# The third sequence's attention scores on the two row halves of TensorE, with a spread mask and a new order of work

## The chip, the core and the metric

The kernel runs on one core of one Trainium2 chip. Five engines work side by side and are tied together by semaphores: TensorE (PE, matmuls; PEld is its weight load), VectorE (DVE), ScalarE (ACT), GpSimd (POOL) and SyncE (SP, here only an issuer of DMA transfers; GpSimd issues others). Each engine carries out its own list of instructions in order. The metric is the device time of one execution in microseconds; the median of three runs before the change is 260.41 us (259.87 to 261.34).

## The reference

Attention over four sequences (batch 4), 8 heads, 768 positions, head dimension 64, with a selection of key chunks, followed by a feed-forward network with squared ReLU:

```python
k_min, k_max = min / max of k over each chunk of 32 keys        # 24 chunks
ub = sum_d maximum(q * k_min, q * k_max)                        # bound of a query on a chunk
ub = where(query_chunk >= chunk, ub, -1e9)
top_chunks = the 6 chunks with the largest ub, for each query
scores = q @ k.T / 8
mask = (chunk of key in top_chunks) & (query >= key)
attn = softmax(where(mask, scores, -1e9))
x = attn @ v                                                    # (3072, 512)
out = relu(x @ w_in) ** 2 @ w_out                               # 512 -> 2048 -> 512
```

## The kernel before

**Tiles.** A sequence has six tiles of 128 positions. The first tile of each of the four sequences (it has only four chunks, fewer than the six that are chosen, so that nothing is left out there) is handled by `first_attention`, and these four tiles share one feed-forward pass ("F"). The other five tiles of sequence b are handled by pairs of heads: pair p = 4 b + hp, so the third sequence (b = 2) is pairs 8 to 11 and the fourth pairs 12 to 15. After its four pairs each sequence has its own feed-forward pass: up groups (four matmuls into one PSUM bank, line 1186), a relu on ScalarE or VectorE (1193, 1195), a square on VectorE (1204), down groups (four matmuls, line 1217).

**Two ways of scoring.** In the old way (`stage_a`, `stage_b`), sequences 0 to 2 here, keys and queries are copied into `kqc` tiles with 64 + 24 rows: 64 of the head, and 24 that hold for each chunk a large negative number on the key side and, on the query side, whether the chunk is *not* selected. One matmul over 88 rows then yields scores that already carry the chunk mask. A head has five PSUM banks of 512 columns (`BANKS`), each filled by two matmuls (line 1026). ScalarE takes the exponential (1050), GpSimd or VectorE cuts the diagonal blocks to their triangle (1006, 1003), and TensorE multiplies by the values (1038). `stage_a` prepares this for a pair: key copies `kc`, chunk minima and maxima (line 862), query parts, query copies `qc`, bounds on TensorE (825, 827), the eight largest (833), the selection `selb` (892), its transpose `sT`, and four copies of it into the `kqc` rows.

In the new way (`stage_a_turned`, `score_banks`, `stage_b_turned`), sequence 3 here, the scores are taken straight from the transposed keys and queries: for each block one matmul over rows 0 to 63 for the first head of the pair and one over rows 64 to 127 for the second (line 1083), which run on the two row halves of the array. `score_banks` does two banks of both heads, 16 matmuls, in one burst. The mask comes another way: the selection is made as large or zero numbers on VectorE (946, 957), transposed by SyncE, written to DRAM (`seen`, line 967), and spread from there by four transfers over 32 partitions each (line 974) into a tile `mask`. GpSimd cuts the mask's diagonal blocks (1006), and VectorE takes the minimum of exponential and mask (`choose`, line 1130). The values matmul is line 1116.

For sequences 2 and 3 keys and queries come already transposed, by SyncE's transposing DMA from tiles that GpSimd has loaded; for these sequences the transposition of the selection is SyncE's too, in both ways of scoring.

**Order.** The program first lists all operations (1797), each with the engines that may run it. `SEQUENCE` is the list of their numbers in the order in which they are issued, with a letter (D, A, G) where an operation may run on more than one engine. So this list fixes the order on each engine and the choice between engines. `Plan.order` walks through it with a model of durations and DMA (`Transfers`); at run time the model's only trace is how the buffers are assigned and how many warm-up matmuls fill the gaps at the start. Due times and leads in `P` were used by the search that made the list; the kernel itself takes from `P` the number and order of the loads (which also numbers the operations) and which passes go by DMA.

**Buffers.** PSUM: one bank `tp`, three `ps`, two `av`, two `ff`. The up and down groups use `ff`. Eight `e` buffers hold exponentials until the values matmul has used them. Three large buffers `set` hold the two `kqc` sets, sequence 1's loaded keys and queries, and later the masks.

Of the kernel before, what the change touches and what calls it, by code (L numbers as in the profile page):

```python
# [9 lines left out]
F32 = mybir.dt.float32  # L10
# [36 lines left out]
4 0 23 1 131 2 18 6 20 8 62D 7 10A 19 150 5A 22 12A 134 136 9A 135D 21 11D 13A 24 14D  # L47
3A 25 132 133D 27 61D 17D 137 16 148 26 138 146 142 147D 31 149D 143 139 174 144 29
151 145 176 140 152 141 32 177D 156 153 188 175A 154 28 157 155 178 15A 158 179 159 33
162 180 190 163D 191A 30 189D 164 184 36 192 195 193D 34 160 196A 198 161D 201 46 197  # L50
199A 194 165 202A 200 185 35 170 181 186 203 166 187 37 182 171 183 172 167 173 40 286
206 168 280 169 207A 287 41 204 290D 205A 39 288 282A 211 289D 208 45 212D 281A 213
214 209D 284 215A 217 60 226 218A 283 51 223 210 285 42 227A 219 291 224A 343 292 220
44 216 345A 293 43 229 294 344A 225 295 221A 347 296 230A 52 235 298A 346 297A 54 232
300A 228 299A 236D 38 309 317 222 310 349 237 301 48 233A 238 350 302 351 47 313 352D
318 241 348 314 353D 50 239A 305 234 322 311G 354 306 240 303G 323 355 250 67 307D 356
242A 315D 326 55 357 251A 304 308 330 324D 358 327 312 316 319 49 252 334 325 243 359
335 244 53 363D 331 362D 361D 412 332G 245A 385 336G 413 338 386 247 328G 360D 56 339
231 415D 372 248A 59 368 253 414 369 320 416D 69 373 376 249 364 406 321 374G 365 380
370G 409 256 254A 366G 65 410 367 371 375 377 389 68 262 381 408D 390 411 329 246 401  # L60
397 407D 391G 333 417 378G 398 337 255 340 469 387G 341 418 393 399G 471A 257 66 419
342 402 379 382 64 420 263 394 421 395D 388 383 422 472 392 71 396 423A 400 403 258
424D 384 435 404 427 426D 264 425D 428 473 436 448 439 449 57 470D 431 259 440 405
429G 432 474 460 437D 441D 475 260A 72 443 476 430 461 265 261 477 433G 444 70 478D
452 480 453 434 268 73 481 479A 483 462D 456 58 482 464 457 269 484 78 465 458D 438
266A 485 442 731 104 486D 267 270 487D 732A 488D 75 489D 506 450D 490 734 507 498 454G
445 271 79 499 735 491 451 98 455 494 500D 459 733D 463 495 523 492G 466 446 511 74
524 467 274 447 512 468 81 272A 737 736 525D 515 739 519 496G 502 741D 520 493 77 497
275 738 503 105 740D 513G 516 742 85 504D 527 743 501 505 528 508 521D 794 517G 509
744 83 514 518 796A 522 526 510 529 276 117 530 99 745 795A 531 277 76 746 797 80 747  # L70
534 278A 63G 749D 535A 532 748D 750D 102 533A 584 760 751D 585A 764 798 539 765 768
542 540A 799 769 800 543D 578 86 761 802 536 90 579A 544 801 752 537A 572 541 82 753
766G 580 756 538 575 573A 803D 805 804D 576A 557 108 84 757 577 545 806 558A 857 574
754G 546A 807 548 762G 858A 89 777 549D 566 808 859A 560 550 547 781 94 809 773 561A
755 860 567A 551 778 758G 103 581 774 562 779G 759 568 763 582D 782 767 785 87 775D
# [65 lines left out]
1755 1753D 1764 1756D 1757 1716 1715 1719 1770 1720A 1765A 1721 1728 1717A 1737 1718  # L141
1771D 1773 1754 1772 1729D 1766 1779 1730 1738D 1758 1780 1759A 1760 1774 1739 1781
1782 1775 1783D 1776 1784 1785 1777D 1786 1778 1787 1788 1791 1789A 1792 1793 1794
1790 1795A 1796
"""


class Transfers:
# [11 lines left out]
    def run(self, queues, until):  # L160
        now = self.now
# [1161 lines left out]
```

## Time and profile before

| | |
|---|---|
| median of 3 runs | 260.41 us |
| profiled execution | 260.51 us |
| its span, first to last instruction | 258.8 us |
| granted TensorE clock | 0.998 |
| scores matmuls, old way (line 1026) | 240 matmuls, 40.6 us busy |
| scores matmuls, new way (line 1083) | 160 matmuls, 6.2 us busy |
| exponentials (lines 1050 and 1121) | 120 x 602 ns and 40 x 602 ns |
| old scores of the third sequence | first at 118.5, last at 165.1 us |
| new scores of the fourth sequence | first at 166.6, last at 205.2 us |

How to read it: "busy" is the time in which an engine had an instruction under way; matmuls are pipelined, and each one's record is longer than the step to the next one, so that the busy time of a group of matmuls is more than what the group adds to TensorE's list. The chain of waits is followed back from the last instruction, and shows what a piece of work really added. A row of a group gives line, engine, operation, names (result, then operands), shape, count, busy us, mean ns of one, and idle time of the engine just before with what ended it.

### The profile page before, as it was taken

Reading aid. Unit: us, or ns where it says so; the run is one execution under the profiler, and the core shown is the slowest. Engines: PE = TensorE matmul, PEld = TensorE weight load, DVE = VectorE, ACT = ScalarE, POOL = GpSimd, SP = SyncE. Lnnn points to the kernel's source line nnn. Section 1 sums busy time; section 2 is a strip of 40 time slices with the busy share of each in tenths; the row PEclk is TensorE's granted clock in tenths of the full one; section 3 lists DMA queues with packets and bytes.
Section 4 is the critical chain, followed back from the end, with each engine's and each line's share of the span. In section 5 each row is a group of like instructions: output and inputs, shape, how many; then the busy total and the mean of one; then the engine's idle time right before and its main releaser. Section 6 shows DMA issues by size and latency. Waiting matters only on the chain.

```text
span 258.8 us, 6699 instructions
## 1 busy us (share of the span) xinstructions
PE 248.7 (96%) x2482; PEld 159.2 (62%) x2482; DVE 202.3 (78%) x719; ACT 177.6 (69%) x352; POOL 113.6 (44%) x194
## 2 busy tenths in 40 slices
PE   8787999999999999999999999999999999999995
PEld 3555466656688666565687656656765654865543
DVE  4659999999999999999999984578978870674630
ACT  7666898598799999999997638766977630421201
POOL 8979899769855599431311304231032200010000
PEclk9999999999999999999999999999999999999999
DMA  9999999999999999994658214973993206120022
GB/s 124 128 163 162 181 171 183 180 163 160 135 177 174 159 132 128 169 123 101 85 166 182 36 25 109 206 91 117 196 188 57 85 11 153 20 81 3 7 93 103
DMA packets 117280, 31.89 MB, mean 123 GB/s; under 512 B 99840, under 2 KB 114944, under 8 KB 117248
## 3 DMA queue, kind: packets, MB, share of 16 engines
q0 software_dynamic: 77968, 16.00, 76.3%
q1 hardware_dynamic: 39280, 15.47, 31.4%
q8 instruction: 19, 0.31, 0.5%
q14 instruction: 13, 0.11, 0.2%
HBM read 32.77 MB, written 6.55 MB: 152 GB/s over the span
## 4 chain that ended last, share of the span: by engine, by line
PE 63%; DMA 14%; DVE 10%; POOL 8%; issue 2%; ACT 1%; POOLq 0%
PE py L1217 27%; PE ph L1186 20%; DMA w_in_sb<-in_moe_w_in_dram 6%; PE ps L1026 6%; PE av L1038 4%; DMA w_out_sb<-in_moe_w_out_dram 3%; DMA qt<-nt 3%; PE ps L1083 2%; DVE kr L862 2%; PE av L1116 2%; DMA nt<-in_q_dram 2%; POOL kn L574 2%; DVE kqc L389 1%; DVE h L1204 1%; POOL q L481 1%
## 5 line engine op out<-in xcount | busy, mean ns | idle before, releaser
L1186 PE MATMUL ph<-xT,w_in_sb 128*128 128x256 bf16 (+2 forms) x592 | 98.1, 304 | 1.6 <-DMA w_in_sb<-in_moe_w_in_dram 0.9
L1217 PE MATMUL py<-w_out_sb,h 128*128 128x512 bf16 (+2 forms) x400 | 93.4, 370 | 0.0
L1050 ACT ACTIVATE e<-ps 128x512 bf16<-128x512 f32 x120 | 66.4, 602 | 9.3 <-PE ps L1026 7.5
L1193 ACT ACTIVATE ht<-ph 128x256 bf16<-128x256 f32 (+2 forms) x102 | 45.1, 451 | 39.4 <-PE ph L1186 30.7
L1186 PEld LDWEIGHTS <-w_in_sb 128*128 128x128 bf16 x592 | 54.8, 97 | 26.0 <-issue 1.3
L1217 PEld LDWEIGHTS <-h 128*128 128x128 bf16 x400 | 37.0, 97 | 33.3
L1204 DVE TENSOR_TENSOR h<-ht 128x384 bf16<-128x384 bf16 (+2 forms) x148 | 46.4, 334 | 10.3 <-ACT ht L1193 9.5
L1006 POOL TENSOR_SCALAR_AFFINE_SELECT e<-e 128x128 bf16<-128x128 bf16 (+1 forms) x68 | 23.2, 352 | 44.5 <-ACT e L1050 44.1
L1026 PE MATMUL ps<-kqc 88*128 88x128 bf16 (+1 forms) x240 | 40.6, 272 | 0.0
L1195 DVE TENSOR_SCALAR ht<-ph 128x384 bf16<-128x384 f32 (+2 forms) x46 | 22.8, 497 | 15.4 <-PE ph L1186 14.6
L1038 PEld LDWEIGHTS <-e 128*128 128x128 bf16 x480 | 23.3, 97 | 6.0 <-POOL e L1006 0.2
L1026 PEld LDWEIGHTS <-kqc 88*128 88x128 bf16 x240 | 19.7, 97 | 10.7 <-DVE kqc L389 0.7
L1121 ACT ACTIVATE e<-ps 128x512 bf16<-128x512 f32 x40 | 21.2, 602 | 5.7 <-PE ps L1083 3.4
L1038 PE MATMUL av<-vn,e 128*128 128x65 bf16 x360 | 23.7, 193 | 0.1
L1006 POOL TENSOR_SCALAR_AFFINE_SELECT mask<-mask 128x256 bf16<-128x256 bf16 x20 | 9.1, 481 | 30.6 <-DMA mask<-seen 30.6
L387 ACT COPY ob<-py 128x512 f32<-128x512 f32 (+2 forms) x18 | 10.2, 564 | 14.2 <-PE py L1217 14.2
L1231 POOL DMA_DIRECT2D out_dram<-ob x10 | 5.6, 556 | 31.9 <-DVE ob L389 18.3
L733 DVE TENSOR_TENSOR x<-av,rc 128x320 bf16<-128x320 f32 (+1 forms) x40 | 18.8, 473 | 0.8
L1130 DVE TENSOR_TENSOR e<-e,mask 128x512 bf16<-128x512 bf16 x40 | 16.1, 438 | 1.6 <-ACT e L1121 1.6
L862 DVE TENSOR_REDUCE kr<-kT 128x24 bf16<-128x768 bf16 x16 | 14.7, 948 | 0.1
L567 POOL DMA_DIRECT2D vn<-in_v_dram x15 | 13.6, 911 | 0.3 <-PE av L1038 0.3
L833 DVE MAX8 m<-ubm 128x8 f32<-128x24 f32 x120 | 12.0, 168 | 0.1
(116 smaller groups left out, 319.5 us busy)
## 6 DMA issues: line engine op xcount, KB each, us to landing
mask<-seen SPq DMA_DIRECT2D x16, 336.0 KB, 6.4
out_dram<-ob SPq DMA_DIRECT2D x13, 256.0 KB, 2.3
out_dram<-ob POOLq DMA_DIRECT2D x10, 256.0 KB, 2.7
w_in_sb<-in_moe_w_in_dram POOLq DMA_DIRECT2D x4, 512.0 KB, 7.6
w_out_sb<-in_moe_w_out_dram POOLq DMA_DIRECT2D x4, 512.0 KB, 9.0
vn<-in_v_dram POOLq DMA_DIRECT2D x15, 128.0 KB, 6.6
nt<-in_q_dram POOLq DMA_DIRECT2D x10, 128.0 KB, 5.1
nt<-in_k_dram POOLq DMA_DIRECT2D x10, 128.0 KB, 6.4
```

Source lines behind the costliest of these rows:

```text
L733: return plan.op({"DVE": 0.06 + 0.00108 * D * n}, due, lambda _: nc.vector.tensor_mul(x(), av[:, :, 0:D], rc[:, 0:n].unsqueeze(2).to_broad ...
L862: nc.vector.tensor_reduce(kr[:, mm].rearrange("d (t c) -> d t c", c=128 // CH) if b >= BY_DMA else kr[:, mm], part(kT).rearrange("d t (c j ...
L1006: nc.gpsimd.affine_select(out=e, in_=e, compare_op=ALU.is_ge, fill=0.0, base=0, channel_multiplier=-1, pattern=[[0, n], [1, 128]])
L1026: nc.tensor.matmul(ps[:, 128 * c:128 * (c + nt)], lhsT=kqs(slice(0, KC), s, hh)[:, 128 * j:128 * (j + 1)], rhs=qss(slice(0, KC), s, hh)[:, ...
L1038: nc.tensor.matmul(av[:, t - 1], lhsT=e[:, 128 * c:128 * (c + 1)], rhs=value_tile(b, h, j), start=(i == 0 and c == 0), stop=(i == len(BANK ...
L1050: nc.scalar.activation(e.tile, ps.tile, ACT.Exp, scale=scale), [sc], [ps, e])
L1121: done = plan.op({"ACT": 0.487}, due + 0.5, lambda _: nc.scalar.activation(e.tile, ps.tile, ACT.Exp, scale=scale), [sc], [ps, e])
L1186: nc.tensor.matmul(ph.tile, lhsT=w_in_sb[:, ki, 128 * f:128 * (f + 1)], rhs=xT[:, c0 // 128:c1 // 128, ki], start=(ki == 0), stop=(ki == N ...
L1193: nc.scalar.activation(ht.tile, ph.tile, ACT.Relu)
L1195: nc.vector.tensor_scalar_max(ht.tile, ph.tile, 0.0)
L1204: {"DVE": 0.075 + w / 1920}, at[0] + P["h2"], lambda _: nc.vector.tensor_mul(h2[f][:, c0:c1], ht.tile, ht.tile), [op], [ht, h2[f]], port=T ...
L1217: nc.tensor.matmul(py.tile, lhsT=h2[f][:, 128 * t:128 * (t + 1)], rhs=w_out_sb[:, f, c0:c1], start=(f == 0), stop=(f == NFI - 1))
```

## The change

The third sequence (pairs 8 to 11) goes the new way, too: `MASKED` falls from 3 to 2. For this sequence there are then no key and query copies, no selection copies and no triangle on the exponentials; instead there are 4 more writes of the selection to DRAM, 16 more spreads of the mask, 20 causal selects of the mask on GpSimd, 40 minima on VectorE and 10 bursts of 16 score matmuls. The output is computed as before.

The bounds of the pairs that go the new way are put in `ff` instead of `tp`. The list of operations has 1787 entries, and `SEQUENCE` is a new one throughout, from its first entries on: the order of the loads, which engine takes which copy, relu and triangle, and where everything stands are new. The model of the transfers has one more constant (a lower rate in the first 10 us), and `P` has other values; several keys in it are read by nothing in the kernel.

```diff
@@ SEQUENCE: all of it replaced; its first line before and after
-4 0 23 1 131 2 18 6 20 8 62D 7 10A 19 150 5A 22 12A 134 136 9A 135D 21 11D 13A 24 14D
+4 0 19 1 131 2 17D 61D 20 18 6 7 21 136 5A 8 23 150 30 13A 15D 134 14A 12D 29 135A 16
...
     SHARED = ((6.2, 0.90), (9.0, 0.95), (1e9, 1.0))
+    EARLY = (10.0, 0.85)
     ISSUED = {True: 0.7, False: 1.3}
...
-            span = min([until - now] + [q[0][1] / rate for q in active])
+            if now < self.EARLY[0]:
+                rate *= self.EARLY[1]
+                until_then = self.EARLY[0] - now + 1e-9
+            else:
+                until_then = 1e9
+            span = min([until - now, until_then] + [q[0][1] / rate for q in active])
...
-             sel=2, loads='K1 Q1 Q3 K3 V0 V1 Q2 K2 i0 V2 k0 V3 q0 i1 k1 v2 q1 i2 '
-             'v0 i3 k2 q2 o1 o0 v1 o2 k3 o3 v3 q3')
...
+    P = dict(... later='q1 k1 v1 k2 v3 q2 k3 v2 q3', ... xt=(1, 2, 3), ub='ff', ...
+             loads='K1 Q1 V1 Q2 V0 K2 Q3 K3 i0 V2 k0 V3 q0 i1 k1 v2 q1 i2 v0 i3 k2 q2 '
+             'o0 v1 o2 k3 o1 o3 v3 q3', out=[1, 2], sel=2)
...
     BY_DMA = 2
-    MASKED = 3
+    MASKED = 2
...
-        ub = buffer("tp", [128, NS, 2, NC], F32, name="ub")
+        ub = buffer("ff", [128, NS, 2, NC], F32, name="ub")
```

Counted by engine from both lists, where they differ in number: on VectorE copies of the selection 26 and 10, triangles on exponentials 28 and 16, query copies 16 and 9, first-tile copies 7 and 2, output copies 7 and 4, FFN input copies 1 and 5, relus 46 and 43, minima 40 and 80; on GpSimd triangles on exponentials 68 and 48, on masks 20 and 40; on ScalarE key copies 16 and 8, relus 102 and 105, output copies 18 and 21; on SyncE spreads 16 and 32, writes of the selection 4 and 8.

In the new list GpSimd's first loads are the first tiles K1, Q1, V1, V0, a pair of k for sequence 0, Q3, K3, V2, K2, Q2, V3, and then the first quarter of w_in; before they were V0, Q1, K1, K3, Q3, V1, Q2 and then the first quarter of w_in. The third sequence's first burst stands after the last scores of sequence 1. Between the third sequence's first mask spread and its first minimum stand, on VectorE, the eight key reductions of the fourth sequence.

More of the change, by code (lines that the diff above doesn't have):

```diff
@@ L145 @@
+1767A 1768 1771 1775 1776 1772 1777 1773D 1778 1774 1781 1779A 1782 1783 1784 1780
+1785A 1786
 """
@@ L164, in run @@
             rate = self.RATE / len(active)
-            span = min([until - now] + [q[0][1] / rate for q in active])
+            if now < self.EARLY[0]:
[4 more added lines that the diff above has]
+            span = min([until - now, until_then] + [q[0][1] / rate for q in active])
             if len(active) > 1:
                 before, share = next(x for x in self.SHARED if now < x[0])
-                span = min([until - now, before - now + 1e-9]
+                span = min([until - now, until_then, before - now + 1e-9]
                            + [q[0][1] / rate / share for q in active])
```

200 lines of the change are left out of this document (95 added, 105 removed).

## Prediction

> **What bounds the kernel now.** First the totals and the slices, then the engines' busy time in three stretches.
>
> ```profile
> span 258.8 us, 6699 instructions
> PE 248.7 (96%) x2482; PEld 159.2 (62%) x2482; DVE 202.3 (78%) x719; ACT 177.6 (69%) x352; POOL 113.6 (44%) x194
> DMA  9999999999999999994658214973993206120022
> ...
> core 0: us, PE busy (x) PEld busy (x) DVE busy (x) ACT busy (x) POOL busy (x), PEclk, DMA share, GB/s
> 0.00:30.00 30.00, 23.95 (x236) 14.34 (x237) 19.83 (x80) 20.42 (x34) 26.14 (x38) 1.00 1.67 148
> 30.00:150.00 120.00, 119.14 (x1285) 80.84 (x1285) 115.83 (x437) 106.49 (x214) 72.02 (x122) 1.00 1.54 146
> 150.00:258.80 108.80, 105.64 (x963) 64.02 (x960) 66.66 (x204) 50.69 (x105) 15.40 (x35) 1.00 0.42 92
> ```
>
> TensorE is busy for 119.1 of the 120 us between 30 and 150, at a granted clock of 1.00. VectorE is busy for 115.8 of the same 120 and has only 4.2 us of room there; after 150 it has 108.8 - 66.7 = 42 us. So TensorE's work sets the end, and VectorE is right behind it in just the stretch where the third sequence's attention runs. The chain of waits says the same in its pieces (start, duration, what):
>
> ```profile
> 150.01 2.59 PE py L1217 x12
> ...
> 154.97 0.44 PE ps L1026 x4
> ...
> 167.24 2.70 PE py L1217 x12
> 169.94 0.55 PE ps L1083 x16
> ```
>
> It runs without holes along TensorE: FFN groups with score matmuls between them. A matmul taken out here is time gained, unless another engine makes TensorE wait.
>
> The profiled execution took 260.51 us: the span of 258.8 and 1.7 around it. The median of the three runs is 260.41, so I work from 260.5 and take off 0.1 at the end.
>
> **The scores.** x4 of L1026 is two heads' banks in the old form: 0.44 us, 0.22 a bank. The third sequence has 40 banks (4 pairs of heads, 2 heads, 5 banks): 8.8 us. x16 of L1083 is four banks in the new form, two heads on the two row halves: 0.55 us, and the twelve FFN matmuls in front of it take 2.70 instead of 2.59, so 0.11 more goes at the switch. Ten such bursts are 10 x 0.66 = 6.6 us. **Gain 2.2 us** on TensorE. The values matmuls, the bounds and the FFN stay as they are.
>
> The Trainium skill's page "TensorEngine Tiling (Array Packing)" (Theoretical Speedup) gives up to 2x where the contracted side is at most 64. By that the 8.8 us would become 4.4 and the sum would be 2.2 us lower than mine. The rows show 8.8 / 6.6 = 1.33x, and I go by the rows.
>
> **VectorE.** The rows, as line, operation, count, busy us, mean ns:
>
> ```profile
> L1130 DVE TENSOR_TENSOR e<-e,mask 128x512 bf16<-128x512 bf16 x40 | 16.1, 438 | 1.6 <-ACT e L1121 1.6
> L862 DVE TENSOR_REDUCE kr<-kT 128x24 bf16<-128x768 bf16 x16 | 14.7, 948 | 0.1
> L389 DVE COPY kqc<-sT 24x256 bf16<-24x256 bf16 (+1 forms) x26 | 7.7, 295 | 1.0 <-PE sT L392 0.4
> L759 DVE TENSOR_REDUCE kr<-kt 128x24 bf16<-128x768 bf16 x8 | 7.5, 945 | 0.0
> L1003 DVE TENSOR_TENSOR e<-e,tri 128x128 bf16<-128x128 bf16 (+1 forms) x28 | 6.9, 254 | 2.6 <-ACT e L1050 2.4
> L389 DVE COPY kqc<-qT 64x640 bf16<-64x640 bf16 x12 | 5.8, 484 | 0.1
> L389 DVE COPY ob<-py 128x512 f32<-128x512 f32 x7 | 4.8, 690 | 6.7 <-PE py L1217 6.7
> L892 DVE TENSOR_TENSOR selb<-ubm,m 128x240 bf16<-128x240 f32 x12 | 4.8, 401 | 0.1
> L946 DVE TENSOR_TENSOR selb<-ubm,m 128x48 bf16<-128x48 f32 (+2 forms) x16 | 3.1, 244 | 0.0
> L389 DVE COPY t<-T 128x512 bf16<-128x512 bf16 x7 | 2.9, 422 | 5.0 <-PE T L392 5.0
> L957 DVE TENSOR_SCALAR selb<-selb 128x168 bf16<-128x168 bf16 x4 | 0.8, 204 | 0.1
> ```
>
> Added: 40 mask minima, 40 x 16.1/40 = 16.1; the finer selection, 3.1 + 0.8 - 4 x 4.8/12 = 2.3. Removed, by counting the engine letters of both lists: copies of the selection on VectorE fall from 26 to 10 (-16 x 0.30 = -4.8), triangular products from 28 to 16 (-12 x 0.25 = -3.0), query copies from 16 to 9 (at 0.48 at most -3.4, some are a shorter form, I take -2.7), first-tile copies from 7 to 2 (-2.1), output copies from 7 to 4 (-2.1). Smaller shifts of the new list (more copies of FFN inputs on VectorE, fewer relus) I take as zero. **Net +3.7 us** on VectorE. Its room between 30 and 150 was 4.2, and it shrinks with what TensorE gains there, to about 2. So 3.7 - 2 = 1.7 us don't fit, unless the new order moves work out of the stretch. It does for some: both key reductions of the very first pair (2 x 0.95) now stand ahead of the first FFN groups, in the 30 - 19.8 = 10 us that VectorE had idle at the start. The price is 0 if that is used in full, 1.7 if not, and up to 4.2 if the little idle time is hand-overs that no order removes. I take 0.5.
>
> The bounds of sequences 2 and 3 move from the one tp bank of PSUM to the two ff banks, where the FFN groups rotate; each holds its bank for one bounds group and one add, about what an up group and its relu hold, eight times in all: price 0. The changed planner constants and due times act only through the list.
>
> ScalarE loses the third sequence's long key copies and gets other copies in return; its 40 exponentials remain, and with 106 of 120 busy it isn't the bound. GpSimd gives up 20 triangular selects on e for 20 on the mask; it has 48 us idle in the stretch, price 0, cover enough.
>
> **SyncE and the mask.** Added are 4 writes of the selection to DRAM and 16 transfers that spread it, and what GpSimd waits for:
>
> ```profile
> 133.37 0.38 SPq L967 DMA_DIRECT2D seen<-sT  x1
> 135.11 3.32 SPq L974 DMA_DIRECT2D mask<-seen  x4
> ...
> 144.85 1.95 POOL L1006 TENSOR_SCALAR_AFFINE_SELECT mask<-mask 128x256 bf16<-128x256 bf16 x4 [7.34 <-DMA mask<-seen]
> ...
> mask<-seen SPq DMA_DIRECT2D x16, 336.0 KB, 6.4
> L1006 POOL TENSOR_SCALAR_AFFINE_SELECT mask<-mask 128x256 bf16<-128x256 bf16 x20 | 9.1, 481 | 30.6 <-DMA mask<-seen 30.6
> DMA to landing us min/median/max: 4.4/6.4/9.2
> ```
>
> From the first of four spreads (135.11) to the start of GpSimd's causal selects (144.85) is 9.7 us; two selects at 0.46 make 10.7 before the first minimum can go. In the new list TensorE has between the first pair's first spread and its first minimum nine FFN down groups (0.86 each: 2.59 / 3), three bursts (0.66), and an up group, a bounds group and four values groups (together about 1.2): 10.9 us. VectorE has all eight key reductions of the fourth sequence there (8 x 0.94 = 7.5) and some 3 us of selections and normalisations besides, so the wait is filled. That fits with 0.2 to spare. The third pair has about as much; the other two have some 2 us more, though their spreads are issued further apart. Queued behind a late minimum on VectorE is everything: the squares of the FFN and the next bounds, and then TensorE. I take 0 for it, with 0 to 4 as bounds. The third sequence's selections were already turned by SyncE before, so nothing is added there; the next sequence's input transposes and the last key tile of sequence 3 queue behind the spreads, each 0.3 to 0.5 of issue, while sequence 1's FFN inputs are ready only after its last values.
>
> **The start.** The list is new throughout. Of its loads, the first quarter of w_in is now 13th of GpSimd's loads instead of 8th, with ten first tiles and two pairs of heads ahead of it instead of seven first tiles:
>
> ```profile
> 8.81 7.81 DMA w_in_sb<-in_moe_w_in_dram
> ...
> 22.00 7.61 DMA w_in_sb<-in_moe_w_in_dram
> ...
> k<-in_k_dram POOLq DMA_DIRECT2D x3, 128.0 KB, 4.0
> kn<-in_k_dram POOLq DMA_DIRECT2D x8, 80.0 KB, 6.5
> ...
> 23.04 4.10 PE L1186 MATMUL ph<-xT,w_in_sb 128*128 128x256 bf16 x24 [0.39 <-ACT xT L387]
> ```
>
> Between the two landings (16.62 and 29.61) the queue moved three first tiles, nine pairs and two weight quarters of 512 KB, 2128 KB, or 164 KB/us. The 544 KB more put the first quarter at 16.6 + 3.3 = 19.9. All four sequences' first-tile attention is ahead of it in the new list, so TensorE has then only FFN groups and one pair's transposes to do. The row of 24 holds four narrow up groups and two of twice their width, so 4.10 / 8 = 0.51 a narrow one; eight of these and about 1 us of transposes and bounds bring the new list to 19.9 + 4.1 + 1 = 25.0. The old list has its eight narrow groups done at 23.04 + 4 x 0.51 = 25.1. I take 0, and -1.0 to +1.2 as bounds.
>
> **Sum.** 260.5 - 2.2 (scores) + 0.5 (VectorE) + 0 (mask, start) = 258.8, less 0.1 against the median: **258.7 us**, its own range 257.2 to 260.0.
>
> **The rivals.**
> *VectorE becomes the pace* (260.4): the 1.7 us that don't fit are paid, with 0.5 more where TensorE stands for a hand-over: 260.5 - 2.2 + 2.2 - 0.1. For it speaks 115.8 of 120; against it that 42 us lie free after 150 and that the fourth sequence's preparation can slide there. The Trainium skill's page named above (PSUM Bottleneck) says that tiling speeds up TensorE and not the emptying of PSUM; the 40 exponentials and, added here, 40 minima after them would be that.
> *The masks come late* (263.5, slower): pairs one and three have under 1 us of slack between first spread and first minimum. If the four spreads take 13 us instead of 9.7, because sequence 3's tiles and sequence 1's input transposes share the 16 engines with them, each of the two stops VectorE and then TensorE for some 2.6 us: 260.5 - 2.2 + 5.2 = 263.5. It decides the sign from about 11.6 us on. For it: the landing of one spread goes from 4.4 to 9.2, and the slices from 110 to 129 us show DMA at 9, 4 and 6 tenths without any spread. Against it: at 136 to 142 us, with four spreads under way, it is 8 tenths and most of that is their own.
> *The new order wins more* (256.9): a start 1.0 earlier and no price on VectorE, 260.5 - 2.2 - 1.0 - 0.1 = 257.2, with some of the switch time hidden 256.9. For it: 6 of the first 30 us have no TensorE work; against it: the first weights come later, not earlier.
> *The new scores gain nothing*, being hidden: TensorE at 119.1 of 120 speaks against, and I give it no chance of its own.
>
> **How the numbers follow.** A measurement of this kernel can tell about 0.5% (1.3 us) from no change, so faster is under 259.1, slower over 261.7. Forecast 0.45 (of it 0.36 faster, 0.09 same), more 0.17 (faster), VectorE's pace 0.16 (0.01 faster, 0.13 same, 0.02 slower), late masks 0.22 (slower, some of it only to the bound: 0.20 slower, 0.02 same). That is 0.54, 0.24 and 0.22. The range leaves out the upper part of the late masks and the lower end of the third rival: 256.7 to 262.3.
>
> **What would show it.** Right: the old scores' line at 160 matmuls and the new scores' line at 320, in 20 bursts; TensorE still over 119 of 120 between 30 and 150; VectorE 3 to 5 us busier in total, with the minima of the third sequence starting within 0.3 us of the mask's last causal select. Wrong: TensorE's idle time ended by minima or by VectorE's squares between 100 and 150 (VectorE's pace, if VectorE shows no idle time there; late masks, if VectorE waits for GpSimd's select on the mask), four spreads over 11.6 us from first issue to last landing, or a first FFN group after 21 us with idle time behind it.

## The result, and the profile after

The changed kernel takes **268.24 us** (median of 4 runs, 267.63 to 268.65) against 260.23 for the kernel before in the same comparison (4 runs, 259.87 to 261.34): ratio 1.030, 95% interval 1.026 to 1.034. It is slower by 8.0 us, outside the predicted range. The span is 266.9 us, before 258.8.

First the totals and the queue of SyncE's transfers (packets, MB, share of the 16 engines) of the changed kernel. Its line numbers are 4 lower than before: 1186 is now 1182, 1217 is 1213, 1026 is 1022, 1083 is 1079, 1130 is 1126.

```profile
span 266.9 us, 6891 instructions
PE 249.8 (94%) x2539; PEld 159.0 (60%) x2564; DVE 205.4 (77%) x735; ACT 173.3 (65%) x347; POOL 115.7 (43%) x195
q1 hardware_dynamic: 50864, 21.11, 44.8%
```

Then the three stretches as before:

```profile
core 0: us, PE busy (x) PEld busy (x) DVE busy (x) ACT busy (x) POOL busy (x), PEclk, DMA share, GB/s
0.00:30.00 30.00, 23.57 (x235) 15.35 (x236) 20.34 (x78) 19.67 (x35) 26.80 (x39) 0.94 1.63 146
30.00:150.00 120.00, 117.59 (x1287) 77.77 (x1298) 114.60 (x415) 97.12 (x196) 70.40 (x117) 1.00 1.71 164
150.00:270.00 120.00, 108.68 (x1021) 65.86 (x1032) 70.45 (x245) 56.52 (x118) 18.50 (x40) 0.98 0.55 112
```

TensorE by its records stands still for 2.4 us between 30 and 150, where it stood for 0.9. Two waits make 1.2 of it (0.7 and 0.5); part of the rest can be matmuls that the trace lacks, since it has 1287 beside 1298 weight loads there. Its time behind 150 has grown by 8.1 us with the span, while its busy time there has grown by 3.0 only (105.64 before). VectorE is busy for 3.1 us more in all, but 1.2 us *less* between 30 and 150 (115.83 before): it has not become the pace. The 0.94 in the first stretch is a low granted clock behind a wait of 1.34 us for a first tile of v (the clock is the third number from the end):

```profile
17.80:21.20 3.40, 3.40 (x37) 2.56 (x36) 1.80 (x7) 1.08 (x2) 2.08 (x3) 0.50 1.84 164
```

It hardly moves the start: in e2_warm below, which starts in the same way and has no such stretch, the first FFN group begins at 21.27 us, here at 21.25.

What TensorE, VectorE and SyncE waited for (engine, line, releaser: total, times, longest):

```profile
PE ph L1182 <- DMA xT<-x: 3.3, 1, 3.3
...
PE av L1112 <- DVE e L1126: 1.2, 1, 1.2
...
PE ub L745 <- DVE qp L777: 0.7, 1, 0.7
...
DVE e L1126 <- POOL mask L1002: 1.9, 1, 1.9
DVE qp L777 <- DMA qt<-nt: 1.3, 1, 1.3
...
SPq L970 <- DMA seen<-sT: 14.1, 5, 5.5
SPq L963 <- DMA sT<-selb: 9.4, 3, 3.9
```

The three waits of TensorE shown here can be followed back to one kind of cause. The FFN input of sequence 2 (`xT`) comes late from SyncE. A value group waits for a minimum, which waits for GpSimd's select, which waits for the mask's spreads. The bound of pair 8 waits for VectorE, which waits for sequence 2's turned queries. All of these are transfers that SyncE issues. But the bound of pair 8 stands at 102.4 us, and the first spread of that pair goes out at 117.15, so the new spreads have no part in this wait. The list of transfers (KB each, median from issue to landing) of the changed kernel shows them slower:

```profile
mask<-seen SPq DMA_DIRECT2D x32, 336.0 KB, 6.7
seen<-sT SPq DMA_DIRECT2D x8, 64.0 KB, 4.7
xT<-x SPq DMA_TRANSPOSE x15, 3.5
qt<-nt SPq DMA_TRANSPOSE x10, 7.4
sT<-selb SPq DMA_TRANSPOSE x8, 5.3
```

and that of the kernel before:

```profile
seen<-sT SPq DMA_DIRECT2D x4, 64.0 KB, 1.8
xT<-x SPq DMA_TRANSPOSE x15, 3.2
qt<-nt SPq DMA_TRANSPOSE x10, 5.9
sT<-selb SPq DMA_TRANSPOSE x8, 2.3
```

The spread itself has hardly changed (6.7, before 6.4). What has more than doubled is what a mask needs *before* its spreads: the transpose of the selection (2.3 to 5.3) and its write (1.8 to 4.7). Where it happens, the timeline of SyncE's issues in the changed kernel shows (start, duration, what):

```profile
166.72 0.86 SPq L963 DMA_DIRECT2D seen<-sT  x1
167.63 6.37 SPq L970 DMA_DIRECT2D mask<-seen  x2
174.04 3.21 SPq L505 DMA_TRANSPOSE xT<-x  x2
```

The write of pair 13's selection goes out at 166.72, behind three spreads of pair 12, and takes 6.8 us to land, where the median of its like in the kernel before is 1.8. The two spreads after it are pair 12's last (at once) and pair 13's first, which can only be issued when that write has landed; so the two take 6.37 us. SyncE's list is in order, and the two input transposes of sequence 2 stand behind. The last values that they need were written by VectorE up to 172.37:

```profile
171.88 0.49 DVE L729 TENSOR_TENSOR x<-av,rc 128x320 bf16<-128x320 f32 x1
```

so the first of them, out at 174.04, is 1.7 us late by SyncE's list. Then the two take 5.5 and 5.2 us to land, where 3.5 is the median, with two spreads issued just ahead of them. On TensorE that is:

```profile
176.90 1.04 PE L1213 MATMUL py<-w_out_sb,h 128*128 128x512 bf16 x3
181.27 0.72 PE L1182 MATMUL ph<-xT,w_in_sb 128*128 128x256 bf16 x4 [3.34 <-DMA xT<-x]
181.79 1.91 PE L1213 MATMUL py<-w_out_sb,h 128*128 128x512 bf16 x4
```

and the same place in stretches:

```profile
177.00:181.00 4.00, 0.88 (x3) 0.20 (x3) 2.54 (x18) 1.35 (x3) 0.92 (x3) 1.00 1.13 182
181.00:185.00 4.00, 3.73 (x24) 2.00 (x26) 1.30 (x4) 1.84 (x4) 0.00 (x0) 0.58 0.96 169
```

A wait of 3.34 us, and right behind it four microseconds at a granted clock of 0.58, in which the same down group takes 1.91 us in place of about 1.0. In this execution the wait costs twice. The 8 us do not hang on the low clock, though: of the four executions of the changed kernel, two have a mean granted clock of 0.987 (268.65 us, the profiled one, and 268.46), one has 0.994 (267.63) and one 0.998 (268.02).

**Where the 8 us arise.** For each of TensorE's operations I take its start and subtract the summed price of all TensorE work ahead of it in its list (0.86 us for a group of four matmuls of 512 columns, 0.22 for an old bank of scores, 0.64 for a burst, and so on, from the usual steps in the traces). What remains is the lag, the time that TensorE has not worked so far, each time in the profiled execution. It grows only where time is lost:

```
TensorE work done, us    20    80   100   130   150   170   all
lag, before            15.7  18.4  19.0  19.5  19.7  19.9  20.4
lag, changed kernel    16.7  19.7  22.2  23.5  25.1  30.7  31.3
lost more, step by step +1.0  +0.3  +1.9  +0.8  +1.4  +5.4  +0.1
```

The sum is 10.9 us lost. TensorE's whole work by the same prices is 232.6 us in place of 235.1, 2.5 less. 10.9 - 2.5 = 8.4, of which the spans show 266.9 - 258.8 = 8.1. By these prices the gain of the scores is there; it is outweighed more than four times. The 1.9 us between 80 and 100 us of work lie ahead of the first new spread (the bound of pair 8 at 102.4 us, and 0.5 us for a triangle on VectorE at 111.9). Of the 1.4 us between 130 and 150, 1.2 are the value group that waits for pair 10's mask. The 0.8 us between 100 and 130 come in pieces of some 0.2 us, and no wait in the list explains them.

### The profile page after: what moved, and what is told of

It reads as the page before. It is cut to its first block, busy times and chain, and to the rows that moved or that the text cites. A ratio compares the mean times of both kernels' runs of the same rounds, so it can differ in the third digit from the quotient of the medians.

```text
span 266.9 us, 6891 instructions
## 1 busy us (share of the span) xinstructions
PE 249.8 (94%) x2539; PEld 159.0 (60%) x2564; DVE 205.4 (77%) x735; ACT 173.3 (65%) x347; POOL 115.7 (43%) x195
## 3 DMA queue, kind: packets, MB, share of 16 engines
q1 hardware_dynamic: 50864, 21.11, 44.8%
## 4 chain that ended last, share of the span: by engine, by line
PE 64%; DMA 13%; DVE 12%; POOL 6%; issue 2%; SPq 1%; ACT 0%; POOLq 0%; DVEq 0%; ACTq 0%
PE py L1213 27%; PE ph L1182 21%; PE ps L1079 4%; PE av L1112 4%; DMA nt<-in_q_dram 3%; DMA kt<-nt 3%; DMA qt<-nt 3%; PE ps L1022 3%; PE av L1034 2%; DMA v<-in_v_dram 2%; DMA xT<-x 2%; DVE h L1200 2%; DVE kr L755 2%; DVE kr L858 1%; DVE kqc L385 1%
## 5 line engine op out<-in xcount | busy, mean ns | idle before, releaser
L1213 PE MATMUL py<-w_out_sb,h 128*128 128x512 bf16 (+2 forms) x375 | 90.1, 373 | 1.3
L1189 ACT ACTIVATE ht<-ph 128x384 bf16<-128x384 f32 (+2 forms) x105 | 47.0, 454 | 31.9 <-PE ph L1182 27.0
L1200 DVE TENSOR_TENSOR h<-ht 128x384 bf16<-128x384 bf16 (+2 forms) x148 | 45.7, 330 | 11.3 <-ACT ht L1189 10.2
L1002 POOL TENSOR_SCALAR_AFFINE_SELECT mask<-mask 128x256 bf16<-128x256 bf16 x40 | 17.4, 470 | 68.0 <-DMA mask<-seen 48.8
L1126 DVE TENSOR_TENSOR e<-e,mask 128x512 bf16<-128x512 bf16 x80 | 33.0, 445 | 8.1 <-ACT e L1117 4.6
L1191 DVE TENSOR_SCALAR ht<-ph 128x256 bf16<-128x256 f32 (+2 forms) x43 | 20.8, 484 | 11.3 <-PE ph L1182 10.9
L1022 PE MATMUL ps<-kqc 88*128 88x384 bf16 (+2 forms) x160 | 26.5, 272 | 0.2
L1002 POOL TENSOR_SCALAR_AFFINE_SELECT e<-e 128x128 bf16<-128x128 bf16 (+1 forms) x48 | 16.8, 364 | 12.3 <-ACT e L1046 11.7
L1112 PEld LDWEIGHTS <-e 128*128 128x128 bf16 x320 | 15.5, 98 | 7.9 <-DVE e L1126 2.0
L1022 PEld LDWEIGHTS <-kqc 88*128 88x128 bf16 x160 | 13.2, 97 | 7.2 <-issue 0.8
L1112 PE MATMUL av<-vn,e 128*128 128x65 bf16 x240 | 17.4, 193 | 0.0
L1034 PEld LDWEIGHTS <-e 128*128 128x128 bf16 x320 | 14.2, 97 | 4.2 <-DVE e L999 0.6
L1034 PE MATMUL av<-vn,e 128*128 128x65 bf16 x240 | 14.6, 193 | 0.5 <-DVE e L999 0.5
```

The lines of the kernel that those rows point to most:

```text
L1002: nc.gpsimd.affine_select(out=e, in_=e, compare_op=ALU.is_ge, fill=0.0, base=0, channel_multiplier=-1, pattern=[[0, n], [1, 128]])
L1022: nc.tensor.matmul(ps[:, 128 * c:128 * (c + nt)], lhsT=kqs(slice(0, KC), s, hh)[:, 128 * j:128 * (j + 1)], rhs=qss(slice(0, KC), s, hh)[:, ...
L1034: nc.tensor.matmul(av[:, t - 1], lhsT=e[:, 128 * c:128 * (c + 1)], rhs=value_tile(b, h, j), start=(i == 0 and c == 0), stop=(i == len(BANK ...
L1112: nc.tensor.matmul(av[:, t - 1], lhsT=e[:, 128 * c:128 * (c + 1)], rhs=value_tile(b, h, j), start=(i == 0 and c == 0), stop=(i == NB - 1), ...
L1126: nc.vector.tensor_tensor(like, like, seen, op=ALU.min)
L1189: nc.scalar.activation(ht.tile, ph.tile, ACT.Relu)
```

## The experiments

The theory: the change puts twice as many masks through SyncE's one list and one queue of transfers, and the new order has no slack for it. The chief rivals: the new scoring costs this much whatever the order (VectorE, clock, busier transfers), or the load order at the start does.

**Taking single waits away.** e1_xt_first moves pair 13's first spread behind sequence 2's two input transposes:

```diff
 SEQUENCE
-... 1451 1505A 1283 1040 1284 1436 1488 1286 1433 1041 1490 1489 1042 1491 1285 1492 ...
+... 1505A 1283 1040 1284 1436 1488 1286 1433 1041 1490 1489 1042 1491 1285 1451 1492 ...
```

> One instruction is moved: SyncE's first mask spread of pair 13, which in the changed kernel waits from 168.6 to 173.7 for its selection to be in DRAM, is issued behind the first two transposes of sequence 2's FFN input instead of ahead of them. Theory S (the place in SyncE's list): the transposes issue some 1.5 us earlier and have less ahead of them in the queue, TensorE's 3.3 us wait at the first up group of sequence 2 is gone and so is the stretch at a granted clock of 0.66 behind it (about 1.9 us): 268.2 - 5.2 = 263.0 us, clock 0.998. Rival (the transposes are late because the DMA engines are full of mask bytes, wherever they stand): the wait stays over 2 us and the time over 266.

Measured: 269.1 us, ratio 1.027 (1.020 to 1.034). The wait shrinks to 0.3 us, as theory S has it, but the time is in the rival's range. At the old place TensorE hardly stops, and the clock stays up (windows of e1_xt_first):

```profile
176.00:181.00 5.00, 4.95 (x46) 2.53 (x44) 3.51 (x27) 0.88 (x2) 1.17 (x3) 1.00 1.31 210
181.00:185.00 4.00, 3.67 (x42) 2.46 (x41) 3.96 (x16) 2.79 (x7) 1.44 (x4) 1.00 1.04 213
```

But the time isn't won. In this execution pair 8's bound waits 2.0 us (0.7 in the changed kernel's, from the same list up to there), two value groups 2.0 instead of 1.2, and one FFN group 1.6. Behind the wait of pair 8's bound the clock falls here, too (the wait, then a stretch of 3.41 us):

```profile
103.90 0.20 PE L745 MATMUL ub<-kbd,qp 128*128 128x48 bf16 x1 [1.96 <-DVE qp L777]
...
105.55:108.96 3.41, 3.41 (x16) 1.65 (x15) 3.34 (x21) 1.60 (x5) 2.45 (x5) 0.50 2.37 96
```

So the places at which the order breaks differ from execution to execution, by some 3 us.

e3_sel_early has that edit, and pair 10's transpose and write of the selection (1106 and 1107) ahead of pair 9's first spread (1087):

```diff
 SEQUENCE, beside e1_xt_first
-... 1069 1087 946 ... 1106 ... 1107 ...
+... 1069 1106 1107 1087 946 ...
```

> As the first of these, and also the transpose of pair 10's selection and its write to DRAM are issued by SyncE ahead of pair 9's four spreads instead of behind them. Theory S: pair 10's spreads can then start some 4 us earlier, its first minimum and the 1.2 us for which TensorE waits at its first values are gone: 263.0 - 1.2 = 261.8 us. Rival (VectorE is late there in any case, or the wait moves to pair 9, whose spreads come later): 263 or more, with the wait at pair 9's first values.

Measured: 268.77 us, ratio 1.032 (1.024 to 1.039). In the profiled execution, the slowest of four at 271.78, value groups wait 2.8 us, an up group 1.9 for VectorE, and another up group 1.5 for its FFN input. The result is the rival's: moving single entries moves the wait.

**The clock.** e2_warm fills the wait for sequence 2's input with matmuls that compute nothing:

```diff
+            if op is self.ops[1287]:
+                op.fill = 15
             if op.fill:
```

> The changed kernel with 30 matmuls of 256 columns (15 fills, 3.2 us) of a constant tile put ahead of the first up group of sequence 2, where TensorE waited 3.3 us for the transposed input. Their result is overwritten. Theory C (the idle time itself brings the granted clock down): the wait is filled, the clock stays at 1.00 in 180 to 185 us, the 1.9 us after it are won: 266.3 us. Rival (the clock falls there for another reason): the clock is 0.6 to 0.7 there again and the time 268.2.

Measured: 271.08 us, ratio 1.036 (1.030 to 1.043). The timeline of TensorE at the same place in e2_warm, whose lines are 2 higher:

```profile
178.20 3.44 PE L656 MATMUL ph<-warm 128*128 128x256 bf16 x30
181.47 0.60 PE L1184 MATMUL ph<-xT,w_in_sb 128*128 128x256 bf16 x4
181.91 1.03 PE L1215 MATMUL py<-w_out_sb,h 128*128 128x512 bf16 x4
```

The transposes come as late as ever, but the groups behind the gap take 0.60 and 1.03 us, where they took 0.72 and 1.91. That fits theory C, the idle time as the cause of the low clock; but it is one execution, and the changed kernel itself has one at 0.998 without any filling. The time missed both expectations. The profiled execution (268.40 us, clock 0.999) is the fastest of the four; the other three have 0.987 and take 271.0 to 271.8 us. The 1.0 us of these two groups was not won in the end time: other waits stood elsewhere.

**Cheaper spreads.** e4_wide_rows keeps the changed kernel's order. The selection is stored in another order of its rows, so that a spread reads one row of 10.5 KB per partition in place of 21 rows of 512 bytes; VectorE chooses tile by tile for it (five choices of 337 ns a pair in place of four of 203):

```diff
...
-            rows = seen[0:8 * NM].rearrange("(u g h) j -> g u (h j)", g=4, h=2)
+            rows = seen[0:8 * NM].rearrange("(g u h) j -> g (u h j)", g=4, h=2)
             nc.sync.dma_start(
-                out=mask[32 * g:32 * g + 32].rearrange("c u h j -> c u (h j)"),
-                in_=rows[g].unsqueeze(0).to_broadcast([32, NM, 2 * 128]))
+                out=mask[32 * g:32 * g + 32].rearrange("c u h j -> c (u h j)"),
+                in_=rows[g].unsqueeze(0).to_broadcast([32, NM * 2 * 128]))
```

> The changed kernel's list, but the selection is written in an order in which each spread reads one row of 10.5 KB for each partition instead of 21 rows of 512 bytes, same bytes; selections on VectorE are one instruction more a pair. Theory B (the length of the spreads, 1.75 us each in the queue, is what the new list has no room for): spreads follow each other in under 1.3 us, the waits at pair 10's first values (1.2 us), at sequence 2's first up group (3.3) and the slow clock (1.9) shrink or go: 262 to 264 us. Rival (the spreads' time is their bytes, not their pieces): 1.7 us or more a spread and 267.5 to 269 us.

Measured: 265.33 us, ratio 1.015 (1.010 to 1.020), 2.9 us below the changed kernel. Both expectations missed: the time lies between them, and the spreads land some 1.5 us apart, not under 1.3 and not at 1.7 or more. The same bytes in fewer packets (30384 in place of 50864) and the transfers of a mask are quicker:

```profile
mask<-seen SPq DMA_DIRECT2D x32, 336.0 KB, 5.5
seen<-sT SPq DMA_DIRECT2D x8, 64.0 KB, 4.1
...
sT<-selb SPq DMA_TRANSPOSE x8, 3.4
```

**Fewer spreads.** e8_few_spreads leaves 12 of the 16 new spreads out, and with them the 15 selects of GpSimd on these masks; pairs 9 to 11 take pair 8's mask:

```diff
-        mask = masks[p] = buffer("set", [128, NM, 2, 128], name="mask")
+        few = 8 < p < 12
+        mask = masks[p] = masks[8] if few else buffer(
+            "set", [128, NM, 2, 128], name="mask")
...
-                     lambda _, g=g: spread_rows(g),
+                     lambda _, g=g: None if few else spread_rows(g),
...
```

> The changed kernel, its order kept, with 12 of its 16 new mask spreads left out, and the minima's diagonal step of the same pairs on GpSimd: pairs 9 to 11 use pair 8's mask, so that their chunk choice is left out of the output. Choosing, its transpose and its write stay, the scores, the exponentials and the minima too. Theory (the transfers of the spreads make the loss behind 100 us): the waits for the mask of pair 10 and for the FFN input of sequence 2 are gone, and the time is 261 to 264, what stays being the start (1.0 us) and the bound of pair 8 (1.7 us). Rival (the new way's work on the engines, or the new order of the loads): 266 to 269.

Measured: 263.72 us, ratio 1.012 (1.005 to 1.019), near the upper end of what the theory expected and below the rival's range. Of 8.0 us, 4.5 hang on these spreads and the selects behind them. The wait for the FFN input of sequence 2 is gone. One is left, for that of sequence 1, whose transposes stand behind the four spreads of pair 8 that stayed:

```profile
PE ph L1189 <- DMA xT<-x: 1.9, 1, 1.9
```

**Another queue.** e6_act_queue issues the spreads from ScalarE's queue:

```diff
-            nc.sync.dma_start(
+            nc.scalar.dma_start(
                 out=mask[32 * g:32 * g + 32]...
...
-        spread = [op({"SP": 0.50}, ...
+        spread = [op({"ACT": 0.10}, ...
```

> The changed kernel with one edit: the four mask spreads of each pair are issued from ScalarE's queue and no more from SyncE's; the order stays. Theory (the small transfers wait behind the spreads' bytes in one queue): the median from issue to landing of the chunk mask's write falls from 4.7 to below 3 us and that of its transpose from 5.3 to below 4, and the time is 262 to 266, with ScalarE stopped at some spreads. Rival (what is shared is the 16 DMA engines, whichever queue a transfer is in): the medians stay above 4 and the time at 267 to 271.

Measured: 275.20 us in the fastest execution (clock 0.986); the other three took 279.4 to 281.4 us at a clock of 0.97 to 0.98, and the trace is of one of these. Both expectations missed the time. The medians of the transfers split the question:

```profile
seen<-sT SPq DMA_DIRECT2D x8, 64.0 KB, 3.2
xT<-x SPq DMA_TRANSPOSE x15, 4.4
sT<-selb SPq DMA_TRANSPOSE x8, 5.0
```

The write no longer stands behind the spreads in its queue and lands in 3.2 us (4.7 in the changed kernel), not quite below the 3 of the theory. The transposes gain next to nothing (5.0; and 4.4 for the inputs, 3.5 in the changed kernel), as the rival has it: the 16 engines are shared, whichever queue the spreads are in. And a new wait stands in ScalarE's list, with everything behind it: the third spread of pair 8 goes out only when the second has landed, 8 us after the first went out. Why it waits for that was not followed; so the time is no clean test of the queue (issues of ScalarE, then waits of ScalarE and of TensorE in e6_act_queue):

```profile
118.45 8.27 ACTq L970 DMA_DIRECT2D mask<-seen  x3
...
ACT e L1117 <- DMA mask<-seen: 8.1, 1, 8.1
...
PE ps L1079 <- ACT e L1117: 5.4, 3, 4.0
```

**Another order.** In e5_list_priced every instruction stays, and the order is searched anew with dearer transfers:

```diff
@@ SEQUENCE: all of it replaced; its first line
-4 0 19 1 131 2 17D 61D 20 18 6 7 21 136 5A 8 23 150 30 13A 15D 134 14A 12D 29 135A 16
+6 18 2 4 26 19 5A 20 174 24 146 23 148 7 21 3A 149D 150 147A 151 134 132 8 160 22
```

> Every instruction of the changed kernel is kept; only the order of the work is another one, searched anew with a mask transfer priced at 1.79 us (the changed kernel's trace shows 1.75 from one landing to the next; its own planner had 1.54) and with SyncE's transposes landing 0.3 to 2.5 us later than that planner had them. Theory (the order left SyncE's list and its transfer queue no slack): the wait for the FFN input of sequence 2 and the wait for a mask are below 1 us each and the time is 260 to 263. Rival (the new scoring costs this much whatever the order, by VectorE's longer work, the busier transfers or the clock): 266 to 269.

Measured: 268.55 us, ratio 1.030 (1.023 to 1.038). The total is the rival's, but its parts are not: the lag is 19.7 at 20 us of work, 3.0 worse than the changed kernel's, and between 100 and all of the work it grows by 5.4 where it grew by 9.1. The search had worsened the start: TensorE's first transpose of a loaded tile starts at 10.5 us, in the changed kernel at 5.3. e7_wide_list adds the wide rows to such an order, with a cheaper way of reordering (the multiplication after the choice does it, from a small buffer of its own):

```diff
...
-            nc.vector.tensor_single_scalar(chosen[:, 0:8 * NM], chosen[:, 0:8 * NM], BIG,
-                                           op=ALU.mult)
+            nc.vector.tensor_single_scalar(
+                chosen[:, 0:8 * NM].rearrange("p (g u h) -> p g u h", g=4, h=2),
+                picks[:, 0:8 * NM].rearrange("p (u g h) -> p g u h", g=4, h=2), BIG,
+                op=ALU.mult)
...
```

> The order is searched anew as in e5_list_priced, now with the chunk mask stored so that a spread reads one row of 10.5 KB per partition (as in e4_wide_rows, where a spread took 1.5 us), and with the choosing left as it was: VectorE's multiplication after it does the reordering. Theory: 258 to 261, no wait above 1 us between 100 and 200 us of the trace. Rival (the new scoring's own price): not below 263.

Measured: 262.94 us, ratio 1.009 (1.005 to 1.012), above the theory's range and just under the rival's bound of 263. The start is bad here too (lag 18.4 at 20); one value group waits 1.4 us.

**The start fixed, rows narrow and wide.** e9_wide_start and e10_start_rows have one and the same order, whose first 320 entries are the kernel before's; e9_wide_start has the wide rows, e10_start_rows the changed kernel's instructions. In e9_wide_start the choices of pairs 10 and 11, and those of 14 and 15, share one buffer at the same time, so that the choice of these pairs isn't the reference's; the work is the same.

> As e7_wide_list (one row of 10.5 KB per partition in a spread, the order searched anew with the measured prices), with the first 320 entries of the order taken from the kernel before, so that the loads and the first sequences' start are as there. Theory (two losses, the start and the masks' transfers, both of them in the order and not in the scoring): TensorE is as early as in the kernel before when it has done 20 us of work (15.7 us behind; 16.7 in the changed kernel), and the time is 257.5 to 260.5. Rival (the scoring on row halves is no gain by itself): 261 or more.

> The same order as e9_wide_start, with the changed kernel's own spreads (rows of 512 bytes) and its own choosing: no instruction differs from the changed kernel, only the order. Theory: a spread takes 1.75 us in place of 1.5, so the time is 1 to 4 us above e9_wide_start and below 264. Rival (the rows matter little where the order leaves slack): within 1 us of e9_wide_start.

Measured: e9_wide_start 260.71 us, ratio 1.000 (0.997 to 1.003), between its theory (up to 260.5) and its rival (from 261); e10_start_rows 268.0 us, ratio 1.025 (1.019 to 1.031). The start is as in the kernel before in both (lag 15.5 and 15.7 at 20), so the 1.0 us of the start was in the first 320 entries, the order of the loads among them. In one and the same order the two are 7.3 us apart, more than either theory said; besides the rows only VectorE's choosing differs, which has as many instructions in both. The order was searched with the price of the wide rows. Whether the narrow rows, with this start and an order searched for them, would do better than 268.0 was not tried. The waits of TensorE for a minimum and the transfers, in e9_wide_start:

```profile
PE av L1115 <- DVE e L1129: 2.2, 2, 2.1
...
mask<-seen SPq DMA_DIRECT2D x32, 336.0 KB, 5.3
seen<-sT SPq DMA_DIRECT2D x8, 64.0 KB, 4.0
```

and in e10_start_rows:

```profile
PE av L1112 <- DVE e L1126: 7.5, 6, 2.3
...
mask<-seen SPq DMA_DIRECT2D x32, 336.0 KB, 7.0
seen<-sT SPq DMA_DIRECT2D x8, 64.0 KB, 5.9
```

Most of it is masks that come late: 7.5 us in six waits in place of 2.2 in two.

**Slack.** e11_margin and e12_margin2 have the wide rows, with two of the small buffers in place of one, and are searched with the spreads landing later still, from two points:

> As e9_wide_start (wide rows in the spreads, the start of the kernel before), the rest of the order searched once more with each spread landing 1.5 us later still, since in e9_wide_start a value waited 2.1 us for pair 9's minimum behind a spread that landed 1.9 us later than the search had it. Theory: no wait above 1 us behind 100 us, and 257.5 to 259.5, below the kernel before: the scoring's gain on TensorE comes out where the masks have slack. Rival (each order only moves the wait): 260 to 262, with a new wait of 1 to 2 us for a minimum or an FFN input.

> A second order found in the same way, from another point (240 entries of the start kept), the same instructions as e11_margin: how much hangs on one lucky order. Theory: within 1.5 us of e11_margin and not above 260.5. Rival (each order only moves the wait): 261 or more.

Measured: e11_margin **259.48 us, ratio 0.996 (0.994 to 0.998)**, the fastest version here, at the upper end of its theory's range, and the only one clearly below the kernel before; e12_margin2 263.28, ratio 1.011 (1.009 to 1.013), which the theory had not above 260.5. The stretch from 100 to 150 in e11_margin

```profile
100.00:150.00 50.00, 49.86 (x583) 32.52 (x582) 47.52 (x189) 40.07 (x84) 13.04 (x30) 1.00 1.39 188
```

and in e12_margin2

```profile
100.00:150.00 50.00, 48.24 (x537) 30.57 (x536) 45.80 (x165) 36.07 (x75) 12.48 (x26) 1.00 1.17 171
```

In the first TensorE loses 0.14 us, in the second 1.76 in small pieces of 0.9 at most. Both orders came from the same search with the same prices, and were expected within 1.5 us of each other. So these prices don't tell a good order from one that is 3.8 us worse; that part of the rival (each order moves the wait) stands.

**What the scoring is worth.** Two controls on the kernel before. e13_before_wide gives it the wide rows alone; e14_before_searched an order searched like e11_margin's, too.

> The kernel before with one edit: its 16 spreads (pairs 12 to 15) read one row of 10.5 KB per partition, and VectorE's multiplication reorders the choice for it. Order and scoring stay. Theory (e11_margin's gain is that of the scoring on row halves): 259.5 to 261.2, no difference that can be told, since the kernel before has hardly a wait for a mask behind 100 us. Rival (e11_margin's gain is that of the wide rows): 258.5 to 259.7.

> The kernel before with wide rows (e13_before_wide), and its order searched anew as that of e11_margin was: the same prices, the first 320 entries kept, the old scoring for sequences 0 to 2. Theory (what e11_margin gains is the scoring's 2.2 to 2.5 us of TensorE work, less what the masks still cost): 259.8 to 261.5, not below e11_margin. Rival (the search gives this to either scoring, and the new one is worth nothing): 258.0 to 259.6.

Measured: e13_before_wide 260.96 us, ratio 1.001 (0.998 to 1.004), so the wide rows by themselves bring the old scoring nothing that can be told. e14_before_searched 260.13, ratio 0.998 (0.996 to 1.000). Both are in their theory's range. Against e11_margin's 0.996 the intervals overlap: whether the new scoring on its own gains some 0.5 us over the old one with an order of equal care, or nothing, stays open.

## Why the prediction was wrong

**The scores: right.** 2.2 us were predicted; by the prices of the lag table TensorE has 2.5 us less work. The old scores' line has 160 matmuls and the new one's 320, as foretold. By the same prices the 40 banks went from 8.9 to 6.4 us, 1.39x. The Trainium skill's page "TensorEngine Tiling (Array Packing)" (Theoretical Speedup) has up to 2x. No run here comes near that.

**VectorE: right in size, and its price was not the matter.** Net +3.7 predicted, +3.1 measured. Some of that is luck: two of the shifts taken as zero cancel each other, copies of FFN inputs (0.4 to 2.1 us) and relus (22.8 to 20.8). VectorE was less busy between 30 and 150 us than before, and stood 1.9 us for a mask at 155, so VectorE's pace did not come about; the 0.5 us taken for it has nothing in the trace that answers to it.

**The start: inside its bounds.** 0 was taken, with -1.0 to +1.2; the lag shows +1.0, and the first FFN group starts at 21.25, behind the 21 named as a mark: the first quarter of w_in, which was to land at 19.9, went out at 13.1 and took 8.0 us. With the kernel before's first 320 entries it is gone (e9_wide_start).

**"SyncE and the mask": this is the step that failed.** It was priced at 0, with 4 as the upper bound. In its place 1.4 + 5.4 = 6.8 us of lag can be followed back to late masks and late input transposes in the profiled execution, and leaving 12 of the 16 spreads out brings 4.5 us of time. (The 1.9 us of lag before, at pair 8's bound, lie ahead of the spreads; they come from the new order, for which the prediction has no term behind the start.) Three things went wrong in it:

- The span of 9.7 us from first spread to select, read from one undisturbed pair of the fourth sequence, was carried over to four pairs in a busier stretch. In the changed kernel the four spreads of pair 8 (first and last issue, then the shortest and longest way to landing) read

```profile
L970 SPq DMA_DIRECT2D mask<-seen x4: 502/512/673, 117.1 to 118.8; - x4
...
DMA to landing us min/median/max: 4.6/6.6/8.9
```

 which is 118.8 + 8.9 - 117.1 = 10.6 us from first issue to last landing, where the prediction's pair took 9.6 by this measure; pair 10's by the same view go out from 143.8 to 145.8 and take up to 10.2, that is 12.2, over the 11.6 that the rival of late masks had as its point. That cost the wait of 1.2 us.
- "Nothing is added there", it said of the selections' transposes. But the transposes and the writes were counted by number only. They are small, and stand in one queue with spreads of 336 KB; their median way to landing went from 2.3 to 5.3 and from 1.8 to 4.7 us. As the next pair's spreads wait for them in SyncE's list, the chain of masks slips from pair to pair.
- Of the transfers behind the spreads only the issue was looked at (0.3 to 0.5 us each; a transpose's takes 1.2 us and more in the trace), and of the FFN inputs only sequence 1's. Sequence 2's stand behind the spreads of the *fourth* sequence's pairs 12 and 13, whose chain has slipped by then. This is the biggest single piece of the profiled execution, 5.4 us: a 3.3 us wait and the low clock behind it. A new user of a queue was judged by the old work beside it, and not by the old work behind it.

**The rival of late masks** had the right sign, the mechanism in part, and 263.5 us; it had two waits of 2.6 us on VectorE, where the loss went mostly past VectorE, through SyncE's list to TensorE. Its chance of 0.22 was too low: every other term had a row behind it, while this one had slack of 0.2 us "to spare" set against an unknown landing time, which is no reason for a price of 0.

What is shown: the transfers of the spreads make more than half of the loss (e8_few_spreads; cheaper ones gain 2.9 us in e4_wide_rows and 7.3 in e9_wide_start against e10_start_rows); one order with slack and cheaper spreads takes the loss back (e11_margin), a second one not wholly (e12_margin2). What stays open beside the scoring's own worth: how the 1.9 us between 80 and 100 of TensorE's work, for the most part the late turned queries of sequence 2, split between the new order of GpSimd's loads and of SyncE's transposes; no run took these apart.

## What to carry to other kernels

When work moves onto a queue, price not only its own transfers but each small one that now stands behind them, and follow the in-order issuer to the next consumer, even when that is another sequence's. A step whose slack is a few tenths of a microsecond against a landing time that varies by several isn't free: price it from the busiest place, not the quietest. And make bulk transfers cheap first (long rows), before an order is searched around them.

## What the runs showed of the hardware

- The length of a transfer's rows matters beyond its own time: the same 21.11 MB in 30384 packets in place of 50864 made 7.3 us in one and the same order (2.9 us in the changed kernel's own), and brought the small writes in the queue from 5.9 to 4.0 us.
- Behind an idle 3.3 us TensorE had about four microseconds at a granted clock of 0.58; with matmuls of no use in the gap its groups kept their usual pace. The Trainium skill's page "TensorE: Matmul & The Clock Gate" (What's actually happening) says that the clock falls to half after an idle window of about 3.4 us and needs about as long of work to come back. The half clock agrees (0.50 from 105.55 to 108.96 us in e1_xt_first, and from 17.80 to 21.20 in the changed kernel), and so does its length, 3.4 us. The length of the gap does not: the longest waits ahead of these two were 1.96 and 1.34 us. A wait of 2.20 us in e4_wide_rows (for a first tile of v, at 18.7 us) left the clock at 1.00; what else decides, no run here shows.
- Transfers issued by another engine still slow SyncE's transposes (5.0 against 5.3 us), though a plain write gets past them (3.2 against 4.7). The Trainium skill's page "DMA: Bandwidth & Descriptors" (Issuing engines are not separate DMA queues) says that the issuers share the same 16 engines. The transposes agree; the write is the part that a queue of its own does help.
